# Spreading q products over the units of the first block, and filling the slots of finished row maxima with halves of a second side product

## The chip, the cores and the metric

The kernel runs on one core of a Trainium2 chip. The metric is the device time of one execution in microseconds (us); each figure for a version is the median of several executions. A profile of one more execution gives the span, from the first to the last instruction of the program, and everything that is read from the trace.

## What is computed

One transformer layer with conditioning: a layer norm whose scale and shift come from `c`, multi-query attention with 32 heads of 16 channels that share one k and one v, a gated residual, a second modulated layer norm, and a bilinear feed-forward part of width 1792.

```python
# x is 2048 x 512; wq 512 x 512; wk and wv 512 x 16; wo 512 x 512
mod = (_silu(c) @ w_mod).reshape(c.shape[0], 6, 1, -1)
sa, ca, ga, sb, cb, gb = (mod[:, 0], mod[:, 1], ...)
h = _layernorm(x) * (1 + ca) + sa
q = heads(h @ wq); k = h @ wk; v = h @ wv
p = _softmax(einsum("bhqd,bkd->bhqk", q, k) * Dh ** -0.5)
x = x + ga * (merge(einsum("bhqk,bkd->bhqd", p, v)) @ wo)
h = _layernorm(x) * (1 + cb) + sb
x = x + gb * (((h @ w_gate) * (h @ w_up)) @ w_down)
```

(The listing is shortened: head splitting and merging stand as `heads` and `merge`.)

## The kernel before

**Units and turns.** The 2048 rows are cut into 4 blocks of 512. Of a block, 4 heads at a time are one *unit*: 8 units a block, 32 in all (`NU`). A unit walks over the 16 tiles of 128 keys (`KT`); one key tile of one unit is a *turn*, so there are 512 turns. In the text "turn 8.3" is turn 3 of unit 8, both counted from 0. `attend` (L1142) writes two turns at a time.

**What a turn holds.** Four kinds of TensorE work, in an order that a string spells out (L48 to L50, read by `attend` at L1149 to L1170):

- `e`: scores of one head against one key tile (`qk_exp`, L631), followed by the exponential on ScalarE (L633). The contraction is 50 rows long, so it uses one half of the array's 128 rows: the digit after the letter says which half (0 or 1). Four a turn.
- `m`: scores for the row maxima of the *next* unit (`max_half`, L1050; product at L581, maximum on VectorE at L584). They run about 30 steps ahead (`LEAD`), two steps a turn. Contraction 48 rows, one half of the array. Four a turn, each followed by one reduction on VectorE. The list of them (`flat`) is used up in turn 30.13, and from there on `max_half` returns at once.
- `x`: one half of a step of a *side product* (`side_half`, L1130, `Group.half`, L506, product at L499). A step is a 128 x 128 by 128 x 512 product; `half` does the 64 rows of one half of the array.
- then, at the turn's end, `pv` (L642): the probabilities of the turn before times v, four products on 32 columns each, over the whole height of the array.

In the second turn of a pair every digit is flipped (L1163), so a side product's halves lie on one half of the array in one turn and on the other in the next. Two neighbours in the string that lie on different halves of the array run at the same time.

**Side products.** A `Group` is one accumulation into one PSUM bank: the q projections (16 of 128 columns by 512 rows, `q_proj` L523, 12 steps or 24 halves each; the first is made whole ahead of the units), the output projection wo (`wo_work`), gate and up of the feed-forward part (`ffn_work`, 28 groups of 12 steps a block) and down (4 groups of 42 steps a block). They stand in the queue `fill`; `cur` is the one in work. Each has a gate: a step number, or that the second layer norm of its block is done (`open_gate`, L1084). What is left when the 512 turns are over is done in `cover` (L1229), in whole steps on the full array height.

**The string chosen.** No side product open: `NO_SIDE`, four `e` and four `m`. A q projection: `FEW`, four side halves a turn. Any other: `MANY`, eight side halves a turn.

**When the rows of a group change.** Both halves of the array add into the same bank, so a half on other rows than the group's last one must come after that one has ended. `Group.half` (L509, L510) makes it wait for an exponential: the one named in `sync["exp"]`. `qk_exp` (L634) sets that name to the first exponential written after any side half. Each engine has its instructions in the order in which they are written.

**Banks.** Eight PSUM banks go round in a ring (L67 to L84): each `e`, `m` and other product takes the next one and gives it back at once, so it waits until the bank's last reader is done. `pv` holds one through a unit and a side group holds one until it is evicted.

**Around it.** A finished q projection is scaled on ScalarE (L528), split into two half-precision parts on GpSimd (L529, L530) and written to memory (L532), from where units read it much later. In the same stretch GpSimd prepares the weights (L905 to L909, L1004 to L1007) that `side_step` loads. `hooks` (L1186) puts wo of a block at step 20 of the next block's first unit, and gate, up and down behind the second layer norm. Eviction: `gate(f)` copies on ScalarE (L816), `up(f)` multiplies on VectorE (L822) and splits on GpSimd (L823, L824).

Of the kernel before, what the change touches and what calls it, by code (L numbers as in the profile page):

```python
# [13 lines left out]
F32 = mybir.dt.float32  # L14
F16 = mybir.dt.float16
AF = mybir.ActivationFunctionType
OP = mybir.AluOpType
# [3 lines left out]
KC = D // 128  # L21
NB = 4
BT = S // NB
UB = H // 4
NU = NB * UB
KT = S // 128
FT = F // 128
# [7 lines left out]
NHF = 12  # L35
V_STEP = 24
M_STEP = 17
Q_BURSTS = {14: 4, 15: 4, 16: 4}

CHANNEL = {0: KC - 1, 3: 0, 4: 1, 6: 2}  # L40
# [6 lines left out]

NO_SIDE = "e0 e1 m0 m1 e0 e1 m0 m1"  # L48
FEW = "e1 m0 e0 x1 m0 x1 e0 x1 m0 x1 e1 m0"
MANY = "x1 e0 x1 m0 x1 e0 x1 e0 x1 m0 x1 m0 x1 m0 x1 e0"  # L50


@with_exitstack
def adaln_mqa_glu_kernel(ctx: ExitStack, tc: tile.TileContext, x_in, wq_in, wk_in, wv_in, wo_in,
                         wg_in, wu_in, wd_in, c_in, wm_in, out):
    nc = tc.nc
# [5 lines left out]
    work = ctx.enter_context(tc.tile_pool(name="work", bufs=2))  # L62
# [73 lines left out]
    for i in range(3):  # L136
        t = consts.tile([128, 2, BT], F16, name=f"sst{i}")
# [342 lines left out]
    ended = []  # L480
    sync = {"due": False, "exp": None}

    class Group:


        def __init__(self, n, op, evict, pre=None):
            self.n, self.op, self.evict, self.prepare = n, op, evict, pre
            self.did, self.p, self.rows = [0, 0], None, None

        def put(self, r0, r1):  # L490
            if self.p is None:
# [14 lines left out]
        def half(self, r):  # L506

            mm = self.put(r, r + 1)
            if self.rows not in (None, r):  # L509
                tc.add_manual_dep(mm.ins, sync["exp"], SYNC)  # L510
            self.rows, sync["due"] = r, True
            if self.ended():
                ended.append(self)

# [8 lines left out]
    def q_proj(b, ch):  # L523

        def evac(p):
            q16 = work.tile([128, 2, BT], F16, name="q16", tag="ev", bufs=3)
            qf = work.tile([128, BT], F32, name="qf", tag="ev", bufs=3)
            nc.scalar.activation(qf, p, AF.Copy, scale=qvs[:, 0:1])  # L528
            nc.gpsimd.tensor_scalar(q16[:, 0, :], qf, 1.0, 0.0, op0=OP.mult, op1=OP.add)  # L529
            nc.gpsimd.tensor_tensor(q16[:, 1, :], qf, q16[:, 0, :], op=OP.subtract)  # L530
            d = dram.tile([128, 2, BT], F16, name=f"qd{b}_{ch}")
            nc.sync.dma_start(d, q16)  # L532
            qd[b, ch] = d

        def op(i):
            k, term = divmod(i, 3)
            wl, hl = TERMS[term]
            return wq[:, wl, k, ch * 128:(ch + 1) * 128], h16[:, hl, k, b * BT:(b + 1) * BT]

        return Group(3 * KC, op, evac)  # L540
# [12 lines left out]
    def max_slots(u):  # L553


        if u == 0:
            slots = [[[("one", r // 4, r % 4, kc)] for _ in range(2)] for kc in range(2) for r in range(8)]
            for r in range(8):
                for a in range(2):
                    slots[-1][a].append(("diff", r // 4, r % 4, 2))  # L560
                slots.append([[("both", r // 4, r % 4, 2)] for _ in range(2)])
            return slots
        return [[[("one", r // 4, r % 4, kc)] for _ in range(2)] for kc in range(4) for r in range(8)]

    flat = [(u, i, last, step) for u in range(NU) for steps in [max_slots(u)]
            for i, step in enumerate(steps) for last in [i == len(steps) - 1]]
# [229 lines left out]
    def ffn_work(b):  # L796

        st = {}

        def op(f, which):  # L800
            def fn(i):
                k, term = divmod(i, 3)
                wl, hl = TERMS[term]
                return W["gu"[which]][:, wl, k, f * 128:(f + 1) * 128], h2s[b][:, hl, k, :]
            return fn

        def pre(f):
            def fn():
                if f == 0:
                    st["glu"] = big.tile([128, 2, FT, BT], F16, name="glu", tag="big")  # L810
            return fn

        def gate(f):
            def fn(p):
                st["g", f] = work.tile([128, BT], F32, name="g", tag="g", bufs=2)
                nc.scalar.activation(st["g", f], p, AF.Copy, scale=2.0 ** -45)  # L816
            return fn

        def up(f):
            def fn(p):  # L820
                gf = work.tile([128, BT], F32, name="gf", tag="gf", bufs=4)
                nc.vector.tensor_tensor(gf, p, st["g", f], op=OP.mult)  # L822
                nc.gpsimd.tensor_scalar(st["glu"][:, 0, f, :], gf, 1.0, 0.0, op0=OP.mult, op1=OP.add)  # L823
                nc.gpsimd.tensor_tensor(st["glu"][:, 1, f, :], gf, st["glu"][:, 0, f, :], op=OP.subtract)  # L824
            return fn

        def dn(t):
            def fn(i):
                f, term = divmod(i, 3)
                wl, hl = TERMS[term]  # L830
                return st["glu"][:, hl, f, t * 128:(t + 1) * 128], W["d"][:, wl, f, :]
            return fn

        def fin(t):
            def fn(p):
                o = x1s[b, t]
                nc.vector.scalar_tensor_tensor(o, p, sca[:, 6:7], o, op0=OP.mult, op1=OP.add)
                r0 = b * BT + t * 128
                nc.sync.dma_start(o_rows[r0:r0 + 128, :], o)
            return fn  # L840

        gu = [g for f in range(FT) for g in (Group(3 * KC, op(f, 0), gate(f), pre(f)), Group(3 * KC, op(f, 1), up(f)))]
        return gu, [Group(3 * FT, dn(t), fin(t)) for t in range(4)]

    def nothing():
        pass
# [192 lines left out]
    mstep = [0, 0]  # L1039
# [38 lines left out]


    fill = deque()  # L1080
    cur = []
    now = [0]

    def open_gate(step):  # L1084
        if not fill:
            return False
        gate = fill[0][0]
        if gate[0] == "h2":
            return gate[1] in h2done
        return gate[0] <= step  # L1090

    side = deque(wlist)
# [10 lines left out]
    qs = deque(q_proj(b, ch) for b in range(NB) for ch in range(KC))  # L1103
    for n in range(LEAD):
# [5 lines left out]
        if n in first:  # L1110
            first[n]()
        for _ in range(Q_BURSTS.get(n, 0)):
            qs[0].whole()
        m, v = n - M_STEP, n - V_STEP
        if 0 <= m < len(mod_rows):
# [11 lines left out]
    fill.extend(([0, 0], q) for q in qs)  # L1127
    nrm = []

    def side_half(r):  # L1130
        while True:
            if not cur:
                if not open_gate(now[0]):
                    return
                cur.append(fill.popleft()[1])
            if not cur[0].ended():
                break
            cur.clear()
        if cur[0].did[r] < cur[0].n:
            cur[0].half(r)  # L1140

    def attend(u, kt):  # L1142


        now[0] = u * NSTEP + 2 * kt
        if cur and cur[0].ended():
            cur.clear()
        side = None if u + kt == 0 else cur[0] if cur else fill[0][1] if open_gate(now[0]) else None
        style = NO_SIDE if side is None else FEW if side in qs else MANY  # L1149
        order = [(w[0], int(w[1])) for w in style.split()]  # L1150
        count = {}
        for turn in range(2):
            now[0] = u * NSTEP + 2 * (kt + turn)
            drain_posts()
            for j, (what, a) in enumerate(order):
                if j == len(order) // 2:
                    for f in ends:
                        f()
                    ends.clear()
                    drain_posts()  # L1160
                    late_max()
                    hooks(u, 2 * (kt + turn))
                a = a if style is NO_SIDE else a ^ turn  # L1163
                if what == "m":
                    max_half(a)
                elif what == "x":
                    side_half(a)
                else:
                    k = count[a] = count.get(a, -1) + 1
                    qk_exp(u, kt + (k // 2 if style is MANY else turn), k % 2, a)  # L1170
            assert not sync["due"]
            for g in ended:
                g.finish()
            ended.clear()
            v = u * KT + kt + turn - 1
            if v >= 0:
                pv(*divmod(v, KT))
                if v % KT == KT - 1:
                    ends.append(lambda: pv_out(u - 1))
            if not late_max() and turns:  # L1180
                _, f, post = turns.popleft()
                f()
                posts.append(post)
            hooks(u, 2 * (kt + turn) + 1)
# [32 lines left out]
    u = NU - 1  # L1217

    pv(u, KT - 1)
    pv_out(u)  # L1220
    if cur:
        for r in range(2):
            while cur[0].did[r] < cur[0].did[1 - r]:
                cur[0].half(r)
        for g in ended:
            g.finish()
    tail = deque([g for g in cur if not g.ended()] + [w for _, w in fill])

    def cover(budget):  # L1229
        while tail and budget > 0:  # L1230
# [24 lines left out]
    gu, down = ffn_work(NB - 1)  # L1255
# [22 lines left out]
```

## Time and profile before

| what | before |
|---|---|
| median of 3 runs | 1716.25 us (1716.1 to 1716.4) |
| span of the profiled execution | 1713.5 us |
| granted TensorE clock over the span | 0.993 |
| TensorE busy | 1666.1 us (97%) |
| VectorE busy | 1393.1 us (81%) |
| ScalarE busy | 1218.4 us (71%) |
| GpSimd busy | 505.1 us (29%) |

The units run from about 97 us to 1539 us; behind them stands the tail, in which the rest of the side products and the whole feed-forward part of the last block are made. In the profile's timeline `sc` is the product of an `e`, `mx` that of an `m`, `side` a side half or step, `mpart` a row maximum, `P` an exponential. The `pv` written in a turn is that of the turn before; a turn is measured from one start of `pv` to the next, and a stretch of turns from the `pv` ahead of it to its last one. A line such as `64*128 64x512` is a product on 64 rows of the array; `128*128 128x512` is a whole step. Busy time of TensorE says little here, since two halves of the array can be busy at once and products are pipelined: starts are compared instead.

### The profile page before, as it was taken

Reading aid. Unit: us, or ns where it says so; the run is one execution under the profiler, and the core shown is the slowest. Engines: PE = TensorE matmul, PEld = TensorE weight load, DVE = VectorE, ACT = ScalarE, POOL = GpSimd, SP = SyncE. Lnnn points to the kernel's source line nnn. Section 1 sums busy time; section 2 is a strip of 40 time slices with the busy share of each in tenths; the row PEclk is TensorE's granted clock in tenths of the full one; section 3 lists DMA queues with packets and bytes.
Section 4 is the critical chain, followed back from the end, with each engine's and each line's share of the span. In section 5 each row is a group of like instructions: output and inputs, shape, how many; then the busy total and the mean of one; then the engine's idle time right before and its main releaser. Section 6 shows DMA issues by size and latency. Waiting matters only on the chain.

```text
span 1713.5 us, 33210 instructions
## 1 busy us (share of the span) xinstructions
PE 1666.1 (97%) x12671; PEld 538.8 (31%) x12671; DVE 1393.1 (81%) x2364; ACT 1218.4 (71%) x2295; POOL 505.1 (29%) x705
## 2 busy tenths in 40 slices
PE   6799999999999999999999999999999999999999
PEld 3223333222223333333333333333323333334444
DVE  7699999999999999999989999999998999604110
ACT  3668888888888777777787777777777777771010
POOL 5724445535576751110020111101011010103130
PEclk9899999999999999999999999999999999999999
DMA  5212122311222210001100000000100000001000
GB/s 201 85 49 81 60 77 72 93 37 56 82 80 60 65 41 9 16 9 29 34 8 19 13 16 9 16 9 16 31 25 22 12 20 5 8 6 45 14 1 25
DMA packets 48939, 66.64 MB, mean 39 GB/s; under 512 B 15302, under 2 KB 29450, under 8 KB 48780
## 3 DMA queue, kind: packets, MB, share of 16 engines
q1 hardware_dynamic: 47196, 64.33, 12.2%
q8 instruction: 99, 1.62, 0.4%
q14 instruction: 60, 0.49, 0.1%
q10 hardware_dynamic: 1584, 0.20, 0.1%
HBM read 51.12 MB, written 8.92 MB: 35 GB/s over the span
## 4 chain that ended last, share of the span: by engine, by line
PE 86%; DVE 8%; ACT 4%; issue 2%; POOL 1%; ACTq 0%; POOLq 0%
PE side L499 49%; PE pv L642 26%; DVE mpart L584 7%; PE sc L631 5%; PE mx L581 3%; ACT P L633 3%; PE pk L257 1%; PE mx L771 1%; PE pq L352 0%; PE mxt L608 0%; PE sc L247 0%; ACT kwb L250 0%; PE misc L871 0%; PE pv L460 0%; PE misc L292 0%
## 5 line engine op out<-in xcount | busy, mean ns | idle before, releaser
L584 DVE TENSOR_REDUCE mpart<-mx 128x1 f32<-128x512 f32 x2016 | 1267.5, 684 | 107.7 <-PE mx L581 103.1
L633 ACT ACTIVATE P<-sc 128x512 f32<-128x512 f32 x2048 | 1093.7, 599 | 269.1 <-PE sc L631 225.7
L631 PE MATMUL sc<-sst,kst 50*128 50x512 f16 x2048 | 661.4, 379 | 0.8 <-DVE mpart L584 0.6
L581 PE MATMUL mx<-kst,sst 48*128 48x512 f16 x2032 | 617.6, 378 | 8.5 <-DVE mpart L584 5.1
L642 PE MATMUL pv<-P,vst 128*32 128x512 f32 x4096 | 546.2, 605 | 1.2
L499 PE MATMUL side<-h2T,wg 64*128 64x512 f16 (+1 forms) x1152 | 278.3, 378 | 1.5 <-ACT P L633 1.5
L499 PE MATMUL side<-h2T,wu 64*128 64x512 f16 (+1 forms) x1144 | 276.2, 378 | 1.0 <-ACT P L633 1.0
L499 PE MATMUL side<-wd,glu 64*128 64x512 f16 (+1 forms) x1008 | 234.0, 378 | 2.7 <-ACT P L633 2.7
L823 POOL TENSOR_SCALAR glu<-gf 128x512 f16<-128x512 f32 x56 | 34.6, 617 | 654.2 <-DVE gf L822 573.2
L631 PEld LDWEIGHTS <-kst 50*128 50x128 f16 x2048 | 174.5, 94 | 130.8 <-issue 109.7
L581 PEld LDWEIGHTS <-sst 48*128 48x128 f16 x2048 | 182.6, 94 | 64.1 <-issue 42.1
L499 PEld LDWEIGHTS <-wg 64*128 64x128 f16 (+1 forms) x1152 | 99.5, 95 | 209.6 <-ACT P L633 99.3
L499 PEld LDWEIGHTS <-wu 64*128 64x128 f16 (+1 forms) x1144 | 99.0, 95 | 201.7 <-ACT P L633 91.3
L642 PEld LDWEIGHTS pv<-P,vst 128*32 128x32 f32 x4096 | 80.8, 108 | 215.8 <-issue 199.7
L499 PEld LDWEIGHTS <-glu 64*128 64x128 f16 (+1 forms) x1008 | 89.1, 95 | 166.3 <-ACT P L633 66.4
L822 DVE TENSOR_TENSOR gf<-side,g 128x512 f32<-128x512 f32 x56 | 38.4, 685 | 124.0 <-PE side L499 91.0
L816 ACT ACTIVATE g<-side 128x512 f32<-128x512 f32 x56 | 33.3, 595 | 96.8 <-PE side L499 96.8
L499 PE MATMUL side<-h,wq 64*128 64x512 f16 (+1 forms) x372 | 97.0, 379 | 0.0
L499 PE MATMUL side<-wo,och 64*128 64x512 f16 (+1 forms) x336 | 79.3, 378 | 0.4 <-ACT P L633 0.2
L824 POOL TENSOR_TENSOR glu<-gf,glu 128x512 f16<-128x512 f32 x56 | 65.2, 1165 | 4.7
L190 POOL TENSOR_SCALAR rv<-st 128x1 f32<-128x1 f32 (+1 forms) x20 | 4.5, 227 | 162.4 <-DVE st L735 146.7
L909 POOL TENSOR_TENSOR kwb<-kwb,wsl 128x448 f32<-128x448 f32 (+1 forms) x40 | 47.5, 1188 | 3.1
(221 smaller groups left out, 773.7 us busy)
## 6 DMA issues: line engine op xcount, KB each, us to landing
wsl<-in_B_w_gate_dram SPq DMA_DIRECT2D x32, 224.0 KB
wsl<-in_B_w_up_dram SPq DMA_DIRECT2D x32, 224.0 KB
wsl<-in_B_w_down_dram SPq DMA_DIRECT2D x28, 256.0 KB
sst<-qd SPq DMA_DIRECT2D x186, 32.0 KB
qd<-q SPq DMA_DIRECT2D x16, 256.0 KB
oc<-ev SPq DMA_DIRECT2D x128, 32.0 KB
rr<-ri SPq DMA_DIRECT2D x16, 256.0 KB
xl<-in_A_x_dram SPq DMA_DIRECT2D x16, 256.0 KB
```

The lines of the kernel that those rows point to most:

```text
L257: nc.tensor.matmul(p, wk3[:, k].rearrange("p a r -> p (a r)"), hf(b, k), start=(k == 0), stop=(k == KC - 1))
L499: return nc.tensor.matmul(self.p, left[64 * r0:64 * r1], right[64 * r0:64 * r1], start=start, stop=self.ended())
L581: nc.tensor.matmul(m, s[64 * a:64 * a + 48, p, t * 128:(t + 1) * 128], keys, start=True, stop=True)
L584: nc.vector.tensor_reduce(part, m, axis=AX.X, op=OP.max)
L631: nc.tensor.matmul(t, kst[64 * a:64 * a + 50, kt * 128:(kt + 1) * 128], s[64 * a:64 * a + 50, p, :], start=True, stop=True)
L633: ex = nc.scalar.activation(ptl[u, kt, p, a], t, AF.Exp)
L642: nc.tensor.matmul(pvb[u][32 * j:32 * j + 32, :], vst[:, kt, :], ptl[u, kt, p, a], start=(kt == 0), stop=(kt == KT - 1))
L816: nc.scalar.activation(st["g", f], p, AF.Copy, scale=2.0 ** -45)
L822: nc.vector.tensor_tensor(gf, p, st["g", f], op=OP.mult)
L823: nc.gpsimd.tensor_scalar(st["glu"][:, 0, f, :], gf, 1.0, 0.0, op0=OP.mult, op1=OP.add)
L824: nc.gpsimd.tensor_tensor(st["glu"][:, 1, f, :], gf, st["glu"][:, 0, f, :], op=OP.subtract)
L909: nc.gpsimd.tensor_tensor(acc, acc, t, op=OP.add)
```

## The change

Three things are changed. First, q projections get two side halves a turn instead of four from key tile 20 on, that is from turn 1.4, through unit 7 (`LIGHT`); from unit 8 on a q projection that is left runs by `MANY`. Second, when the list of row maxima is used up, the `m` slots of `MANY` take halves of a second group, `second`, beside `cur`; when `cur` ends, the second group takes its place, if it was not used in the same turn. Third, what this needs: gate and up of a pair may end in either order (`factor`, `product`), down waits until all gate and up groups are ended (`needs`), and both groups are finished at the end.

```diff
+FULL_Q = 20
...
 FEW = "e1 m0 e0 x1 m0 x1 e0 x1 m0 x1 e1 m0"
+LIGHT = "e1 m0 e0 x1 m0 m1 e0 x1 e1 m0"
 MANY = "x1 e0 x1 m0 x1 e0 x1 e0 x1 m0 x1 m0 x1 m0 x1 e0"
...
-            self.rows, sync["due"] = r, True
+            self.rows, self.turn, sync["due"] = r, now[0], True
...
-        def gate(f):
+        def factor(f):
             def fn(p):
+                if ("g", f) in st:
+                    return product(f, p)
                 st["g", f] = work.tile([128, BT], F32, name="g", tag="g", bufs=2)
                 nc.scalar.activation(st["g", f], p, AF.Copy, scale=2.0 ** -45)
             return fn
...
+        for g in down:
+            g.needs = gu
...
-    cur = []
+    cur, second = [], []
...
-        gate = fill[0][0]
+        gate, group = fill[0]
+        if not all(g.ended() for g in group.needs):
+            return False
...
-    def side_half(r):
+    def side_half(r, cur=cur):
         while True:
             if not cur:
-                if not open_gate(now[0]):
+                if cur is not second and second and second[0].turn != now[0]:
+                    cur.append(second.pop())
+                elif open_gate(now[0]):
+                    cur.append(fill.popleft()[1])
+                else:
                     return
-                cur.append(fill.popleft()[1])
...
-        style = NO_SIDE if side is None else FEW if side in qs else MANY
+        style = NO_SIDE if side is None else MANY
+        if side in qs and u < UB:
+            style = FEW if u * KT + kt < FULL_Q else LIGHT
...
-                if what == "m":
+                if what == "m" and mstep[a] >= len(flat) and style is MANY:
+                    mstep[a] += 1
+                    side_half(a, second)
+                elif what == "m":
                     max_half(a)
```

At the end of the units the old code evened out the two halves of `cur`; the new code does so for `cur` and `second`.

More of the change, by code (lines that the diff above doesn't have):

```diff
@@ L487, in __init__ @@
             self.n, self.op, self.evict, self.prepare = n, op, evict, pre
-            self.did, self.p, self.rows = [0, 0], None, None
+            self.did, self.p, self.rows, self.needs = [0, 0], None, None, ()
         def put(self, r0, r1):
@@ L817, in gate, with product @@
             return fn
[L819 to L825, printed above, removed]
+        def product(f, p):
+            gf = work.tile([128, BT], F32, name="gf", tag="gf", bufs=4)
+            nc.vector.tensor_tensor(gf, p, st["g", f], op=OP.mult)
+            nc.gpsimd.tensor_scalar(st["glu"][:, 0, f, :], gf, 1.0, 0.0, op0=OP.mult, op1=OP.add)
+            nc.gpsimd.tensor_tensor(st["glu"][:, 1, f, :], gf, st["glu"][:, 0, f, :], op=OP.subtract)
         def dn(t):
@@ L840, in fin @@
             return fn
-        gu = [g for f in range(FT) for g in (Group(3 * KC, op(f, 0), gate(f), pre(f)), Group(3 * KC, op(f, 1), up(f)))]
-        return gu, [Group(3 * FT, dn(t), fin(t)) for t in range(4)]
+        gu = [g for f in range(FT) for g in (Group(3 * KC, op(f, 0), factor(f), pre(f)), Group(3 * KC, op(f, 1), factor(f)))]
+        down = [Group(3 * FT, dn(t), fin(t)) for t in range(4)]
+        for g in down:
+            g.needs = gu
+        return gu, down
     def nothing():
@@ L1220, in adaln_mqa_glu_kernel @@
     pv_out(u)
-    if cur:
+    begun = cur + second
+    for g in begun:
         for r in range(2):
[L1223 to L1227, printed above, removed]
+            while g.did[r] < g.did[1 - r]:
+                g.half(r)
+    for g in ended:
+        g.finish()
+    tail = deque([g for g in begun if not g.ended()] + [w for _, w in fill])
     def cover(budget):
```

## The prediction

> **What bounds the kernel now.** I read the page first: its engine sums and its 40 slices.
>
> ```profile
> span 1713.5 us, 33210 instructions
> PE 1666.1 (97%) x12671; PEld 538.8 (31%) x12671; DVE 1393.1 (81%) x2364; ACT 1218.4 (71%) x2295; POOL 505.1 (29%) x705
> ...
> PE   6799999999999999999999999999999999999999
> ...
> DVE  7699999999999999999989999999998999604110
> ...
> L816 ACT ACTIVATE g<-side 128x512 f32<-128x512 f32 x56 | 33.3, 595 | 96.8 <-PE side L499 96.8
> ```
>
> TensorE is busy everywhere, VectorE until the maxima run out. Neither says which sets the pace of a stretch (the last row, a gate's copy, is used below), so next come busy times of stretches that begin and end at a start of pv: 64 turns by FEW from 1.1 on, turns 5.12 to 7.15 (36 without a side product), 8.0 to 8.9 (10, also without), and 16 turns by MANY from 10.1 on.
>
> ```profile
> core 0: us, PE busy (x) PEld busy (x) DVE busy (x) ACT busy (x) POOL busy (x), PEclk, DMA share, GB/s
> 140.20:305.27 165.07, 164.93 (x1350) 52.30 (x1349) 162.32 (x275) 140.69 (x276) 80.62 (x83) 1.00 0.24 74
> 330.54:421.51 90.97, 84.88 (x616) 21.62 (x615) 90.56 (x166) 76.52 (x150) 43.91 (x51) 1.00 0.18 53
> 421.51:445.52 24.01, 22.79 (x161) 5.55 (x160) 23.98 (x41) 21.21 (x42) 16.34 (x21) 1.00 0.30 90
> 516.01:562.19 46.18, 46.08 (x381) 14.19 (x382) 42.08 (x69) 36.70 (x70) 29.89 (x38) 1.00 0.19 55
> ```
>
> With what falls between turns, FEW takes 165.07/64 = 2.58 us a turn, no side product 90.97/36 = 2.53 and 2.40, MANY 46.18/16 = 2.89. In the two stretches without side products VectorE is busy 99.5% and more of the time; it sets the pace there. So q halves under FEW cost almost nothing, while a turn that goes to MANY costs nearly half a microsecond.
>
> What bounds a FEW turn is seen in the timeline of TensorE and, for one reduction, of VectorE:
>
> ```profile
> 161.47 0.39 PE L581 MATMUL mx<-kst,sst 48*128 48x512 f16 x1
> 162.56 0.37 PE L631 MATMUL sc<-sst,kst 50*128 50x512 f16 x1
> 162.67 0.37 PE L581 MATMUL mx<-kst,sst 48*128 48x512 f16 x1
> 162.97 1.07 PE L642 MATMUL pv<-P,vst 128*32 128x512 f32 x8
> 163.97 0.39 PE L581 MATMUL mx<-kst,sst 48*128 48x512 f16 x1
> ```
>
> ```profile
> 161.92 0.69 DVE L584 TENSOR_REDUCE mpart<-mx 128x1 f32<-128x512 f32 x1
> ```
>
> The period is 163.97 - 161.47 = 2.50 us. Partners in other pairs start within 0.01 us of each other, but the last mx starts 0.11 after its partner sc. It starts 0.06 after the end of the reduction of the turn's *first* mx (161.92 + 0.69 = 162.61). That is a ring: first mx, 0.45 to its reduction, 0.69 of reduction, 0.06 of release, last mx, 0.30 to pv, 1.00 of pv, next first mx: 0.45 + 0.69 + 0.06 + 0.30 + 1.00 = 2.50. The cause is in the program: with pv and a side group holding a bank each, six banks go round, a turn takes eight, and the turn's last m gets the bank of its first. Without a side group seven go round, and this tie is gone:
>
> ```profile
> 362.23 1.07 PE L642 MATMUL pv<-P,vst 128*32 128x512 f32 x8
> 364.62 1.06 PE L642 MATMUL pv<-P,vst 128*32 128x512 f32 x8
> ```
>
> The period is 2.39, four reductions of 0.60 each.
>
> **The change, part by part.** The counts are from the order of instructions of the two programs; turns not named here hold the same work in both.
>
> *FEW to LIGHT, turns 1.4 to 5.11 (72).* Two side halves a turn go. LIGHT keeps the m's at the second and the last place and eight bank users a turn, and in the new program the last m again waits for the reduction of the turn's first. So the ring of 2.50 stands and the removed pair of slots (0.22) only becomes a longer wait at the last m: 0 us. If the ring did not bind, VectorE would, at 2.39: -0.11 x 72 = -8. I take 0, as the wait is written in the program and its four durations are rows; -8 stays for the range.
>
> *No side product to LIGHT, turns 5.12 to 7.15 (36).* A side group now holds a bank there too, so the turn goes from 2.39 towards 2.50. By the pure periods that is 36 x 0.11 = +4.0. By the averages with all extras it is 36 x 2.58 - 90.97 = +1.9, but this stretch has single reductions for the weight scales that the first 64 turns lack. I take +3.
>
> *No side product to MANY, turns 8.0 to 8.9 (10).* The 72 q halves that no longer fit run here, ahead of wo: 10 x 2.89 - 24.01 = +4.9.
>
> What moves with them: every q product from the fourth on ends later, with its copy on ScalarE, two operations on GpSimd and a 256 KB store on SP. The last four end between turns 7.15 and 8.9, where weights are split.
>
> ```profile
> 162.11 0.62 POOL L529 TENSOR_SCALAR q<-qf 128x512 f16<-128x512 f32 x1 [6.99 <-ACT qf L528]
> 162.81 1.16 POOL L530 TENSOR_TENSOR q<-qf,q 128x512 f16<-128x512 f32 x1
> 421.86 0.64 POOL L1005 TENSOR_SCALAR wsl<-wsl,sca 128x448 f32<-128x448 f32 x1 [6.70 <-DMA wsl<-in_B_w_gate_dram]
> ```
>
> Four times 1.78 is 7 us more on GpSimd, which has 24.01 - 16.34 = 7.7 us free in ten old turns and 5 more in the longer new ones. But GpSimd may stand up to 6.70 us for a weight load with a q split behind it, SP then holds later loads behind the q store, and ScalarE's next q copy waits for that split in front of exponentials. Three turns lie between two copies, some 8.6 us, which covers such a wait; uncovered it costs up to the difference between 6.70 + 1.78 and that, near 0, and a few us if two such waits chain: 0 to +3, I take 0. The buffers that q's operands free are next written 20 turns later.
>
> *The m slots, from turn 30.12.* 72 side halves leave the tail, 36 whole steps in number (24 are left there instead of 60). A step's price is read in the tail, twelve to a group:
>
> ```profile
> 1542.06 2.75 PE L499 MATMUL side<-h2T,wg 128*128 128x512 f16 x12
> 1544.64 2.75 PE L499 MATMUL side<-h2T,wu 128*128 128x512 f16 x12
> 1547.23 2.75 PE L499 MATMUL side<-h2T,wg 128*128 128x512 f16 x12
> ```
>
> (1547.23 - 1542.06)/24 = 0.215, so 36 x 0.215 = -7.8 us. The Trainium skill, "TensorE: Matmul & The Clock Gate", section "Back-to-back issue gap", gives about 131 ns for sustained 512-column products; by it the saving would be 4.7 and the sum 3.1 worse. The trace has 215, and that decides.
>
> Against it stands a wait. In 18 turns (30.14 to 31.15) the order is x e x, then the second group's first half of the turn, on other rows than in the turn before. It therefore waits for `sync["exp"]`, and that name was set a moment ago by the first e of the *same* turn; the new program shows exactly this wait. Everything TensorE has left of the turn is queued behind it. How long it is:
>
> ```profile
> 1512.06 1.07 PE L642 MATMUL pv<-P,vst 128*32 128x512 f32 x8
> 1513.06 0.39 PE L499 MATMUL side<-h2T,wg 64*128 64x512 f16 x1
> 1513.07 0.39 PE L631 MATMUL sc<-sst,kst 50*128 50x512 f16 x1
> ...
> 1513.29 0.38 PE L499 MATMUL side<-h2T,wg 64*128 64x512 f16 x1
> ...
> 1514.15 0.81 PE L499 MATMUL side<-h2T,wg 64*128 64x512 f16 x3
> 1514.89 1.07 PE L642 MATMUL pv<-P,vst 128*32 128x512 f32 x8
> ```
>
> ```profile
> 1513.49 0.60 ACT L633 ACTIVATE P<-sc 128x512 f32<-128x512 f32 x1 [0.66 <-PE sc L631]
> 1510.73 0.60 ACT L633 ACTIVATE P<-sc 128x512 f32<-128x512 f32 x1 [0.72 <-PE sc L631]
> ...
> 1169.32 0.61 ACT L633 ACTIVATE P<-sc 128x512 f32<-128x512 f32 x1
> ```
>
> ```profile
> 1510.24 0.39 PE L631 MATMUL sc<-sst,kst 50*128 50x512 f16 x1
> ...
> 1169.98 0.39 PE L499 MATMUL side<-h2T,wu 64*128 64x512 f16 x1 [0.25 <-ACT P L633]
> ```
>
> The first exponential starts 0.42 or 0.49 after its sc (by turns; mean 0.46), takes 0.60, and a waiting side half starts 0.05 after the end of the exponential it waits for (1169.98 against 1169.32 + 0.61): the second group's half starts 1.11 into the turn. Behind it on its half of the array stand e e, three second halves and the last e, at a pitch of 0.217 (1513.06 to 1514.15 is five): the last starts at 1.11 + 6 x 0.217 = 2.41 instead of 7 x 0.217 = 1.52, and pv 0.30 after it. The old period is 1514.89 - 1512.06 = 2.83; the new one is 2.83 + 0.89 = 3.72. 18 x 0.89 = +16. Even if the other half of the array ran on during the wait, this chain would stay. Bounds: 0, if the exponential had ended by then, and, if a gate's copy of 0.60 stood before the first exponential in six of the turns, +16 + 3.6. I take +16. Late next is the fourth exponential, but the longer turn gives ScalarE more room than it loses.
>
> *Sum:* 0 + 3 + 4.9 - 7.8 + 16 = +16, so the span goes from 1713.5 to 1729.6. The runs shown have a median 2.75 above that span; 1716.25 + 16 = **1732 us**.
>
> **Rivals.**
>
> *A LIGHT turn runs at VectorE's 2.39.* For it: VectorE is 98% busy under FEW. Against: the ring above. Then the first part is -8, the second 0: -8 + 4.9 - 7.8 + 16 = +5, 1721.
>
> *The new wait is free* (the other side). The place is the fourth product of the last 18 turns: if the exponential's end were not behind the half's turn in TensorE, the slots would be filled at no cost. The sum is 3 + 4.9 - 7.8 = 0, 1716, no measurable change; it decides below 0.17 us a turn (18 x 0.17 = 3.1). For it: in the old kernel the first side half of a turn waits for an exponential too, and mostly pays nothing, as pv covers it. Against: here the exponential is 1.06 after its sc and only two slots (0.43) lie between, and the row at 1169.98 shows such a wait stopping TensorE.
>
> *Both of these:* 5 - 16 = -11, 1705, faster.
>
> *The slots stay empty* can't be: the new order holds 72 more halves there.
>
> **How the numbers follow.** My forecast 0.78, LIGHT at 2.39 0.10, the wait free 0.07, both 0.03; 0.02 is left for a gain that I have not seen. A measurement of this kernel tells 0.2%, 3.4 us, from no change: slower 0.78 + 0.10 = 0.88, same 0.07, faster 0.03 + 0.02 = 0.05. The range reaches down to the first rival, 1721, and up by the queue's 3 and part of the gate copies, 1737; my forecast's own part of it is 1728 to 1737.
>
> **What would show it.** Right: starts of pv 2.50 apart in unit 3 and in unit 6; 46 us for the 16 turns from 8.0; 3.7 apart in unit 31, with a gap of 0.6 to 0.9 before a side product, put down to an exponential; 24 steps of gate and up ahead of the last block's down. Wrong: 2.39 in unit 3 (first rival), 2.8 in unit 31 (second), or a wait of ScalarE for GpSimd near 430 us. I am wrong too if a turn by MANY with q differs from one with gate and up.

## The result and the profile after

| what | before | after |
|---|---|---|
| median of 4 runs each | 1716.2 us (1716.1 to 1716.4) | 1735.17 us (1734.72 to 1735.64) |
| ratio to before | | 1.0113 [1.01, 1.0127] |
| span of the profiled execution | 1713.5 us | 1733.3 us |

The change makes the kernel 19 us slower; 1732 was forecast. The page of the changed kernel (the line numbers shown here are two higher than before: L501 is the side product, L635 the exponential, L644 `pv`):

```profile
span 1733.3 us, 33256 instructions
PE 1674.8 (97%) x12709; PEld 538.3 (31%) x12709; DVE 1397.5 (81%) x2364; ACT 1221.9 (70%) x2295; POOL 504.9 (29%) x705
...
L501 PE MATMUL side<-h2T,wg 64*128 64x512 f16 (+1 forms) x1168 | 285.5, 378 | 7.5 <-ACT P L635 7.5
L501 PE MATMUL side<-h2T,wu 64*128 64x512 f16 (+1 forms) x1166 | 285.1, 378 | 4.4 <-ACT P L635 4.3
```

The sums of the engines look like those of before: TensorE stands at 97% in both. What has changed is the last column of the side products, the idle time ahead of them: 7.5 and 4.4 us, put down to the exponential, where it was 1.5 and 1.0. These 9.4 us more, summed over the whole span, are over half of what the new wait will turn out to cost.

Where the 19.8 us of span went is read from the same stretches as before, cut again at starts of `pv`. After (columns: stretch and its length, then busy time and count of TensorE, its weight loads, VectorE, ScalarE and GpSimd, granted clock, DMA share, GB/s):

```profile
145.23:331.72 186.49, 181.59 (x1366) 53.31 (x1365) 183.28 (x307) 154.77 (x304) 82.04 (x82) 1.00 0.23 69
331.72:428.12 96.40, 92.56 (x687) 26.89 (x686) 94.11 (x166) 77.90 (x154) 47.34 (x55) 1.00 0.19 57
428.12:457.01 28.89, 28.61 (x234) 8.79 (x233) 25.64 (x42) 23.92 (x46) 19.16 (x24) 1.00 0.31 95
1497.75:1565.49 67.74, 58.19 (x433) 15.51 (x431) 3.41 (x7) 43.59 (x79) 7.09 (x8) 1.00 0.01 3
1565.49:1733.30 167.81, 164.03 (x777) 74.68 (x776) 29.77 (x48) 17.15 (x27) 36.09 (x64) 1.00 0.07 22
```

Two of the stretches of before that were not shown yet:

```profile
145.44:330.53 185.09, 184.95 (x1509) 58.54 (x1508) 182.13 (x307) 157.67 (x310) 92.52 (x94) 1.00 0.25 78
...
1486.02:1537.49 51.47, 51.19 (x362) 15.18 (x361) 2.73 (x6) 40.66 (x78) 5.31 (x6) 1.00 0.02 4
```

| stretch | before, us | after, us | difference | forecast |
|---|---|---|---|---|
| turns 1.4 to 5.11 (72) | 185.09 | 186.49 | +1.4 | 0 |
| turns 5.12 to 7.15 (36) | 90.97 | 96.40 | +5.4 | +3 |
| turns 8.0 to 8.9 (10) | 24.01 | 28.89 | +4.9 | +4.9 |
| turns 8.10 to 30.13 (356) | 1040.49 | 1040.75 | +0.3 | 0 |
| turns 30.14 to 31.15 (18) | 51.47 | 67.74 | +16.3 | +16 |
| from the last turn's `pv` on | 176.03 | 167.81 | -8.2 | -7.8 |

The sum is +20.0 before rounding; what is ahead of turn 1.4 gave 0.2 back, which leaves the 19.8 of the span.

**The ring of banks** stands in a `LIGHT` turn as it did in a `FEW` turn. TensorE, and one reduction of VectorE, after (columns: start and length in us, engine, line, operation, tiles):

```profile
160.25 1.07 PE L644 MATMUL pv<-P,vst 128*32 128x512 f32 x8
...
161.25 0.39 PE L583 MATMUL mx<-kst,sst 48*128 48x512 f16 x1
...
162.45 0.37 PE L583 MATMUL mx<-kst,sst 48*128 48x512 f16 x1
162.75 1.07 PE L644 MATMUL pv<-P,vst 128*32 128x512 f32 x8
```

```profile
161.71 0.69 DVE L586 TENSOR_REDUCE mpart<-mx 128x1 f32<-128x512 f32 x1
```

From first mx to its reduction 0.46, reduction 0.69, release 0.05, last mx, 0.30 to `pv`, 1.00 of `pv`: 2.50, although two side halves a turn are gone.

**The new wait**, in unit 31: first TensorE, then the exponential it waits for.

```profile
1539.37 1.06 PE L644 MATMUL pv<-P,vst 128*32 128x512 f32 x8
1540.37 0.39 PE L501 MATMUL side<-h2T,wg 64*128 64x512 f16 x1
1540.37 0.39 PE L633 MATMUL sc<-sst,kst 50*128 50x512 f16 x1
1540.59 0.38 PE L501 MATMUL side<-h2T,wg 64*128 64x512 f16 x1
1541.45 0.39 PE L501 MATMUL side<-h2T,wu 64*128 64x512 f16 x1 [0.48 <-ACT P L635]
1541.45 0.39 PE L501 MATMUL side<-h2T,wg 64*128 64x512 f16 x1
...
1542.76 0.38 PE L633 MATMUL sc<-sst,kst 50*128 50x512 f16 x1
1543.07 1.07 PE L644 MATMUL pv<-P,vst 128*32 128x512 f32 x8
```

```profile
1540.80 0.60 ACT L635 ACTIVATE P<-sc 128x512 f32<-128x512 f32 x1 [0.67 <-PE sc L633]
```

The order in the program is x e x, then a half of the second group (wu). Two products start at 1540.37, one at 1540.59, and then nothing starts until 1541.45, which is 0.05 after the exponential's end (1540.80 + 0.60 = 1541.40). The bracket shows only 0.48 us, because the product of 1540.59 is still running for 0.38; from start to start it is 1541.45 - 1540.59 = 0.86, where the slots around it are 0.22 apart. So an idle column understates such a wait; the forecast had named a gap of 0.6 to 0.9 there. The turn lasts 1543.07 - 1539.37 = 3.70.

**The tail**, after, from the end of the last turn:

```profile
1567.35 0.39 PE L501 MATMUL side<-h2T,wg 64*128 64x512 f16 x1
...
1572.21 10.52 PE L501 MATMUL side<-wd,glu 128*128 128x512 f16 x48
1582.57 10.52 PE L501 MATMUL side<-wo,och 128*128 128x512 f16 x48
```

What is left of gate and up takes 1572.21 - 1567.35 = 4.86 us. In all, gate and up now have 1168 + 1166 side instructions where they had 1152 + 1144: 38 whole steps were made as two halves instead. A step of the tail takes (1582.57 - 1572.21)/48 = 0.216, and 38 x 0.216 = 8.2.

**The turns that were not foreseen.** When all row maxima of a unit are in, VectorE combines them (`mm`, L603) and TensorE transposes the result (`mxt`, L610); `attend` asks for this in the middle and at the end of each turn (`late_max`), and it is due when the count of `m` steps on half 1 of the array reaches a mark. In `FEW` all four `m` of a turn lie on one half, in `LIGHT` three on one and one on the other, so the mark is reached at another place. Such a turn in unit 3, before:

```profile
252.90 1.07 PE L642 MATMUL pv<-P,vst 128*32 128x512 f32 x8
253.90 0.28 PE L608 MATMUL mxt<-ident,mm 128*16 128x128 f32 x1
...
255.83 1.06 PE L642 MATMUL pv<-P,vst 128*32 128x512 f32 x8
```

and after, TensorE and then VectorE:

```profile
250.72 1.07 PE L644 MATMUL pv<-P,vst 128*32 128x512 f32 x8
...
252.16 0.38 PE L583 MATMUL mx<-kst,sst 48*128 48x512 f16 x1
253.17 0.28 PE L610 MATMUL mxt<-ident,mm 128*16 128x128 f32 x1 [0.63 <-DVE mm L603]
...
254.13 1.06 PE L644 MATMUL pv<-P,vst 128*32 128x512 f32 x8
```

```profile
250.28 2.59 DVE L586 TENSOR_REDUCE mpart<-mx 128x1 f32<-128x512 f32 x4
252.90 0.22 DVE L603 TENSOR_REDUCE mm<-mpart 128x16 f32<-128x64 f32 x1
```

Before, the transpose stands behind a `pv` and follows it at once; the turn takes 255.83 - 252.90 = 2.93. After, it stands in the middle of the turn ahead, TensorE has nothing in front of it to do, and waits 0.63 us for VectorE, which has four older reductions to finish first. That turn, 3.13, takes 254.13 - 250.72 = 3.41. It is the interval that starts at the 12th `pv` of the unit's own, called the 12th interval below, and that of each of the units 1 to 7 looks like this (3.42 five times, 3.61 and 3.64).

### The profile page after: what moved, and what is told of

It reads as the page before. It is cut to its first block, busy times and chain, and to the rows that moved or that the text cites. A ratio compares the mean times of both kernels' runs of the same rounds, so it can differ in the third digit from the quotient of the medians.

```text
span 1733.3 us, 33256 instructions
## 1 busy us (share of the span) xinstructions
PE 1674.8 (97%) x12709; PEld 538.3 (31%) x12709; DVE 1397.5 (81%) x2364; ACT 1221.9 (70%) x2295; POOL 504.9 (29%) x705
## 4 chain that ended last, share of the span: by engine, by line
PE 80%; DVE 12%; ACT 5%; issue 2%; DMA 1%; POOL 0%; SPq 0%; ACTq 0%; POOLq 0%; DVEq 0%
PE side L501 45%; PE pv L644 24%; DVE mpart L586 11%; PE sc L633 4%; ACT P L635 4%; PE mx L583 3%; PE pk L259 1%; DMA wmA<-in_w_mod_dram 1%; PE mx L773 1%; PE mxt L610 0%; PE pq L354 0%; PE sc L249 0%; DMA rc<-rs 0%; ACT kwb L252 0%; SPq L658 0%
## 5 line engine op out<-in xcount | busy, mean ns | idle before, releaser
L635 ACT ACTIVATE P<-sc 128x512 f32<-128x512 f32 x2048 | 1097.1, 599 | 293.3 <-PE sc L633 230.6
L633 PE MATMUL sc<-sst,kst 50*128 50x512 f16 x2048 | 688.0, 378 | 4.0 <-ACT P L635 0.4
L583 PE MATMUL mx<-kst,sst 48*128 48x512 f16 x2032 | 609.2, 378 | 4.2 <-DVE sst L265 1.6
L644 PE MATMUL pv<-P,vst 128*32 128x512 f32 x4096 | 545.5, 605 | 0.9
L501 PE MATMUL side<-h2T,wg 64*128 64x512 f16 (+1 forms) x1168 | 285.5, 378 | 7.5 <-ACT P L635 7.5
L501 PE MATMUL side<-h2T,wu 64*128 64x512 f16 (+1 forms) x1166 | 285.1, 378 | 4.4 <-ACT P L635 4.3
L501 PE MATMUL side<-wd,glu 64*128 64x512 f16 (+1 forms) x1008 | 234.1, 378 | 2.8 <-ACT P L635 2.7
L633 PEld LDWEIGHTS <-kst 50*128 50x128 f16 x2048 | 181.4, 94 | 132.3 <-issue 103.0
L583 PEld LDWEIGHTS <-sst 48*128 48x128 f16 x2048 | 177.4, 94 | 76.9 <-issue 55.2
L501 PEld LDWEIGHTS <-wg 64*128 64x128 f16 (+1 forms) x1168 | 100.6, 95 | 214.7 <-ACT P L635 108.4
L501 PEld LDWEIGHTS <-wu 64*128 64x128 f16 (+1 forms) x1166 | 100.0, 95 | 203.6 <-ACT P L635 100.2
L644 PEld LDWEIGHTS pv<-P,vst 128*32 128x32 f32 x4096 | 81.0, 108 | 215.7 <-issue 199.9
L501 PEld LDWEIGHTS <-glu 64*128 64x128 f16 (+1 forms) x1008 | 89.3, 95 | 166.5 <-ACT P L635 66.5
L501 PE MATMUL side<-h,wq 64*128 64x512 f16 (+1 forms) x372 | 122.2, 383 | 0.3 <-ACT P L635 0.3
L501 PE MATMUL side<-wo,och 64*128 64x512 f16 (+1 forms) x336 | 79.3, 378 | 0.3 <-ACT P L635 0.2
L531 POOL TENSOR_SCALAR q<-qf 128x512 f16<-128x512 f32 x16 | 9.9, 617 | 143.2 <-ACT qf L530 143.2
```

The source lines that it names most:

```text
L501: return nc.tensor.matmul(self.p, left[64 * r0:64 * r1], right[64 * r0:64 * r1], start=start, stop=self.ended())
L583: nc.tensor.matmul(m, s[64 * a:64 * a + 48, p, t * 128:(t + 1) * 128], keys, start=True, stop=True)
L633: nc.tensor.matmul(t, kst[64 * a:64 * a + 50, kt * 128:(kt + 1) * 128], s[64 * a:64 * a + 50, p, :], start=True, stop=True)
L635: ex = nc.scalar.activation(ptl[u, kt, p, a], t, AF.Exp)
L644: nc.tensor.matmul(pvb[u][32 * j:32 * j + 32, :], vst[:, kt, :], ptl[u, kt, p, a], start=(kt == 0), stop=(kt == KT - 1))
```

## The experiments

All were timed against the kernel before, beside it on the same chip (its medians there: 1716.14 for the first four, 1715.43 for the last four).

**1. `own_exp`: is it the exponential of the same turn?** The changed kernel, but each group waits for the first exponential written after *its own* last half. That is still an exponential behind that half, and it lies in the turn before.

```diff
-                tc.add_manual_dep(mm.ins, sync["exp"], SYNC)
+                tc.add_manual_dep(mm.ins, self.exp, SYNC)
...
+            waiting.add(self)
...
+            for g in waiting:
+                g.exp = ex.ins.name
+            waiting.clear()
```

> The changed kernel, but each side group waits for the first exponential written after its own last half, not for the one that any group set last. Theory (the wait for the first exponential of the same turn costs 0.89 us in each of 18 turns): the turns 30.14 to 31.15 fall from 3.76 to 2.83 or 2.90 us each, and the time falls by 16 us, to 1719. Rival (the second group's halves are slow by themselves, or its bank makes the scores wait): the turns stay above 3.4 us and the time above 1729.

Measured: 1719.26 us (1718.53 to 1720.0), ratio 1.0018 [1.0008, 1.0027]. The last 18 turns take 51.56 us, with 433 products as in the changed kernel. TensorE in a turn of unit 31:

```profile
1538.67 1.06 PE L650 MATMUL pv<-P,vst 128*32 128x512 f32 x8
1539.67 0.39 PE L503 MATMUL side<-h2T,wu 64*128 64x512 f16 x1
...
1539.90 0.38 PE L503 MATMUL side<-h2T,wg 64*128 64x512 f16 x1
...
1541.51 1.06 PE L650 MATMUL pv<-P,vst 128*32 128x512 f32 x8
```

The second group's half (wg) now starts 0.23 after the turn's first product, and the turn takes 2.84. All 16 us are gone with the halves still in their slots: it was this wait and not the halves.

**2. `light_only`: the change without the second group.** The `m` slots stay empty when the maxima are used up.

```diff
-                if what == "m" and mstep[a] >= len(flat) and style is MANY:
-                    mstep[a] += 1
-                    side_half(a, second)
-                elif what == "m":
+                if what == "m":
```

> The changed kernel without the second group: the m slots stay empty when the maxima are used up. Theory (the LIGHT turns and the ten turns moved to MANY cost 11 to 12 us by themselves): 1728 us, with the last 18 turns at 2.83 us and 60 steps of gate and up left in the tail, as before the change. Rival (the whole loss comes from the end): 1716 to 1719.

Measured: 1727.15 us (1726.96 to 1727.65), ratio 1.0065 [1.0048, 1.0082]. The last 18 turns and the tail are back at 51.38 and 176.05 us. The change falls into two losses: q projections at two halves a turn cost 11 us (1727.15 - 1716.14), the second group another 8.0 (1735.17 - 1727.15; forecast 16 - 7.8 = 8.2).

**3. `second_own_few`: the second group alone, with its own exponential.** As `own_exp`, and q projections as before the change.

```diff
-            style = FEW if u * KT + kt < FULL_Q else LIGHT
+            style = FEW
```

> The second group with each group's own exponential, and q projections by FEW as before the change. Theory: the 36 steps leave the tail (7.8 us), the turns 30.14 to 31.15 cost 0 to 1.2 us more than before: 1708.5 to 1709.5 us, faster than both kernels. Rival (side halves in the m slots cost TensorE time of their own, 0.22 each): no gain, 1716.

Measured: 1707.87 us (1707.12 to 1708.02), ratio 0.9951 [0.9936, 0.9966], a little below the expected range. The page's first line and the last 18 turns:

```profile
span 1705.3 us, 33280 instructions
```

```profile
1485.97:1537.52 51.55, 51.33 (x433) 15.98 (x431) 3.41 (x7) 40.94 (x79) 7.10 (x8) 1.00 0.02 4
```

The same 18 turns take 51.55 where they took 51.47 before, with 433 products instead of 362: the slots are free, and the tail's 8.2 us are a pure gain. This version is faster than the kernel before and than the changed one.

**4. `bank_held`: does the count of banks set a turn?** The kernel before, with one bank taken out of the ring and never written, in the turns without a side product of units 5 to 8.

```diff
+        if style is NO_SIDE and 5 <= u <= 8 and not idle:
+            idle.append(ps_hold("idle"))
+        elif style is not NO_SIDE and idle:
+            ps_give(idle.pop())
```

> The kernel before the change, with one PSUM bank held, and nothing written to it, in the turns without a side product from 5.12 to 8.9; no other change. Theory (a turn is tied by the ring of banks): six banks go round as under FEW and LIGHT, and with the order e e m m e e m m the last m now waits for the turn's second exponential: 0.42 + 0.49 + 0.60 + 0.05 = 1.56 into the turn, 0.32 to pv, 1.00 of pv = 2.88 us instead of 2.39; 46 turns, +22 us, 1738. Rival (VectorE alone sets those turns, and LIGHT is slower because of its side halves): 2.39, 1716.

Measured: 1736.77 us (1735.81 to 1737.04), ratio 1.0119 [1.0104, 1.0134]. One turn of unit 6:

```profile
369.24 1.07 PE L642 MATMUL pv<-P,vst 128*32 128x512 f32 x8
...
371.36 0.86 PE L581 MATMUL mx<-kst,sst 48*128 48x512 f16 x2 [0.30 <-ACT P L633]
372.15 1.07 PE L642 MATMUL pv<-P,vst 128*32 128x512 f32 x8
```

Not one instruction of the turn was added, and it takes 2.91 instead of 2.39. In the order e0 e1 m0 m1 e0 e1 m0 m1 with six banks, the last two `m` get the banks of the turn's first two `e`, whose readers are exponentials, and there the bracket finds the wait. So the bank alone can set the turn, and the order decides which reader it waits for.

**5. `late_max_at_end`: the transposes.** As `light_only`, but in `LIGHT` turns the transposes are not written in the middle.

```diff
-                    late_max()
+                    if style is not LIGHT:
+                        late_max()
```

> The changed kernel without the second group, and in the turns with q halves the row-maxima transposes stay behind pv at the turn's end instead of in its middle. Theory: the 3.42 us turns (the 12th of units 1 to 7) are long because TensorE stands about 0.5 us for the last reductions ahead of those transposes, with nothing behind it to cover that; with the transposes behind pv they fall back to about 2.93, 7 x 0.49 = 3.4 us less than light_only's 1727.15: 1723.7. Rival: the half microsecond comes from the order of the m steps and not from the transposes' place: 1727, and the 12th turns stay at 3.42.

Measured: 1722.18 us (1719.26 to 1722.9), ratio 1.0036 [1.0023, 1.0049], against light_only's 1.0065. Unit 3 again:

```profile
252.46 1.06 PE L644 MATMUL pv<-P,vst 128*32 128x512 f32 x8
253.46 0.28 PE L610 MATMUL mxt<-ident,mm 128*16 128x128 f32 x1
...
255.31 1.07 PE L644 MATMUL pv<-P,vst 128*32 128x512 f32 x8
```

The transpose again follows a `pv` at once; the 12th interval is 2.50 and the 13th 2.84 (255.31 - 252.46 = 2.85), where `light_only` had 3.42 and 2.50. That is 0.58 a unit, 4.1 us in seven, a little more than expected; the span falls by 4.9. Most of the rest is one turn of unit 6 (3.16 against 2.59) that I did not follow up.

**6. `skip_first_slot`: the wait or the halves?** The changed kernel, with the second group kept out of the first `m` slot of a turn. The expectation counts one half too few: a turn goes from four halves of the second group to three.

```diff
-                    side_half(a, second)
+                    if j > 3:
+                        side_half(a, second)
```

> The changed kernel, but the second group leaves the first m slot of a turn empty, so it issues two halves a turn where it issued three. Theory (the wait on the latest exponential issued sets these turns): the first half of a turn then waits for the third exponential of the same turn, later than before, and the last exponential and pv go with it: up to 4.0 us a turn where it was 3.7, in most of the turns 30.14 to 31.15, although a third of their halves is gone; total 1736 to 1740. Rival (the halves' own 0.22 us each make the turns long): 3.5 us a turn, total about 1731.

Measured: 1733.69 us (1733.51 to 1734.04), ratio 1.0107 [1.0092, 1.0122], between the two. TensorE in unit 31, then the exponentials of its first turn shown:

```profile
1538.49 1.06 PE L644 MATMUL pv<-P,vst 128*32 128x512 f32 x8
...
1541.61 0.39 PE L501 MATMUL side<-h2T,wg 64*128 64x512 f16 x1 [0.87 <-ACT P L635]
...
1542.57 1.06 PE L644 MATMUL pv<-P,vst 128*32 128x512 f32 x8
...
1545.18 1.06 PE L644 MATMUL pv<-P,vst 128*32 128x512 f32 x8
...
1547.80 1.06 PE L644 MATMUL pv<-P,vst 128*32 128x512 f32 x8
```

```profile
1539.97 1.57 ACT L635 ACTIVATE P<-sc 128x512 f32<-128x512 f32 x3
```

The half starts 0.07 after the third exponential's end (1539.97 + 1.57 = 1541.54). Where the second group's half waits, the turn takes 1542.57 - 1538.49 = 4.08, longer than 3.70 though it holds a half less, about the size that the theory gave. The rival's 3.5 is not the rule anywhere: one turn, 31.2, takes 3.60, but it was longer than its neighbours before the change too (3.13 against 2.83). But in unit 31 only every third turn waits like that; the next two take 2.61 and 2.62. In the first of them only three side products are made, since the first group has no rows left on this half of the array; in the second the second group is a new one, which has nothing to wait for. The theory of the wait holds, my count of the turns that have it did not.

**7 and 8. `light_order_bare` and `light_order_bank`: q halves, order or bank?** The kernel before, with the order of `LIGHT` but without its side halves, in the turns without a side product of units 5 to 8; the second also holds a bank as in experiment 4.

```diff
+BARE = "e1 m0 e0 m0 m1 e0 e1 m0"
...
+        if style is NO_SIDE and 5 <= u <= 8:
+            style = BARE
```

> The kernel before, with the turns without a side product of units 5 to 8 in the order e1 m0 e0 m0 m1 e0 e1 m0 (that of the turns with two q halves, but with no half in it) and no bank held: seven banks go round. Theory (the count of banks sets the turn, not the order): the last m step waits for an exponential of the same turn, at most 2.43 us a turn where it was 2.39; with the row-maxima transposes in the middle of a turn in three or four units (0.5 us each) about 1719.5 us. Rival (the order sets the turn): 2.50 us a turn, about 1723.

> As light_order_bare, with one bank held and never written in those turns: six go round, as in the turns with q halves. Theory: 2.50 us a turn as in those, though no half is issued: stretch 5.12 to 7.15 at about 96 us (the changed kernel has 96.4), and with the turns of unit 8 about 1722.5 us in all. Rival (the q halves themselves make up part of the 0.11 us): 2.43 to 2.45 us a turn, no more than light_order_bare's 1719.5.

Measured: 1717.62 us (1716.33 to 1718.66), ratio 1.0013 [1.0003, 1.0023], and 1721.01 us (1718.34 to 1722.17), ratio 1.0031 [1.002, 1.0042]. Two starts of `pv` in unit 6, first with seven banks, then with six:

```profile
359.42 1.07 PE L643 MATMUL pv<-P,vst 128*32 128x512 f32 x8
...
361.85 1.06 PE L643 MATMUL pv<-P,vst 128*32 128x512 f32 x8
```

```profile
359.38 1.06 PE L643 MATMUL pv<-P,vst 128*32 128x512 f32 x8
...
361.88 1.07 PE L643 MATMUL pv<-P,vst 128*32 128x512 f32 x8
```

2.43 and 2.50, to the hundredth what the theory gave. The totals came out 1.5 to 2 us lower than expected: the kernel before was 0.8 lower in these runs, and I had put too much on the transposes. Turns 5.12 to 7.15 take 95.40 us with the bank held, against 96.40 in the changed kernel and 92.56 without: three quarters of what the change costs there beyond the order come from a bank that nobody writes.

## Why the forecast was right, point by point

- **The wait of the second group's half: right.** Forecast 1.11 us into the turn, measured 1541.45 - 1540.37 = 1.08; from there six slots to the last `e` (1.31, forecast 6 x 0.217), 0.31 to `pv`. 3.70 and 3.76 by turns where 3.72 was forecast, 16.3 us in all. Experiments 1 and 6 show that it is this wait; the rival in which it costs nothing falls with the 3.70.
- **The tail: right, a little short.** 38 steps left it and not 36: in turns 30.12 and 30.13, over which the list of maxima runs out, two `m` slots each were free already (two `mx` a turn before and after, and two side products more after), which is four halves. A step took the 0.216 that the trace of before gave, 8.2 us in all. With the 131 ns of the Trainium skill, "TensorE: Matmul & The Clock Gate", section "Back-to-back issue gap", 38 steps would have been worth 5.0 us, as an estimate; the trace does not agree.
- **No side product to `MANY`: right**, +4.9. GpSimd's queue made no new wait on the path: there its three q splits waited for ScalarE and not ScalarE for them, as the view of waits for 425 to 460 us has it (total, times, longest; ScalarE's waits there are for TensorE alone):

```profile
POOL q L531 <- ACT qf L530: 16.5, 3, 9.7
```

- **The ring of banks: right.** 2.50 with q halves, without them and with an unwritten bank in their place (experiments 4, 7 and 8). The rival in which a `LIGHT` turn runs at VectorE's 2.39 is refuted.
- **`FEW` to `LIGHT` at 0, and no side product to `LIGHT` at +3: too low**, by 1.4 and 2.4. The step that failed is the sum over pure periods: the first part put "the ring of 2.50 stands" down for all 72 turns, the second came from 2.39, 2.50 and an average, and no term stands for the turns with a transpose. The ring does stand, but the transposes moved from behind `pv` to the middle of the turn ahead, about 0.58 us in each of seven units. Experiment 5 puts them back, and the stretches become 183.78 and 94.14 us: -1.3 and +3.2 against before. The +3 was thus near for the ring alone, though it had been picked between 4.0 and 1.9, so that its closeness is luck in part; against the 0 stands a small gain, which is about that of the third turns of the units 2 to 5 (2.52 instead of 2.74 or 2.94). Why these are shorter was not tried.
- In sum +16 was forecast and +19.8 of span measured. The difference is those two terms; what the others were off by (+0.3, +0.3, -0.4, -0.2) cancels. That 1735 still lies within the range of 1721 to 1737 is luck in part: its upper end had been set for GpSimd's queue and the gate copies, and what came was the transposes.

## What to carry to other kernels

An ordering point that one group shares with another ("the last exponential") becomes a wait on work of the moment as soon as a second group uses it: give each its own, and the same slots go from 16 us lost to nothing. Where a ring of banks is shorter than a turn's users, look up which instruction's reader holds the bank of the last user; filling or emptying slots in between changed nothing here (2.50 with four side halves a turn, with two and with none). And when a string of work is reordered, follow the rare pieces that hang on a count in it, not only the pieces in the string.

## What the runs showed of the hardware

- A half-height product that waits holds up those for the other half of the array too: from 1540.59 to 1541.45 neither half began a product, though the next one for the other half (wg at 1541.45) started together with the one that waited.
- TensorE went on 0.05 us after the end of what it waited for, be it the exponential (1541.40 to 1541.45) or VectorE's `mm` (253.12 to 253.17), and 0.07 in experiment 6 (1541.54 to 1541.61).
- Four `e` and four `m` a turn, in two orders (the second also swaps the halves of the array every other turn) and with seven or six banks: 2.39 us (order of before, seven banks), 2.91 (the same, six), 2.43 (order of `LIGHT`, seven), 2.50 (the same, six). One bank costs 0.52 us in the one order and 0.07 in the other.
